# A hand-laid order for VectorE and ScalarE in the first two blocks of a retention-plus-MLP kernel

## The chip, the cores and the metric

The kernel runs on one core of a Trainium2 chip. The time of a kernel is the device time of one execution in microseconds (us); medians and ranges over several executions are given. A run counts as slow when it takes over 1.5% longer than the fastest of the same kernel; every timed run told here was in the other, fast state, except one single look whose state can't be known and from which no total time is compared. "The profile" is one recorded execution. Its engines are TensorE (PE, with its weight loads as PEld), VectorE (DVE), ScalarE (ACT), GpSimd (POOL) and SyncE (SP).

## The reference

```python
# attention: batch 4, 8 heads, 768 steps, head_dim 64
gamma = 1.0 - 2.0 ** (-5.0 - np.arange(H))
for t in range(S):
    state = gamma * state + einsum('bhd,bhe->bhde', k[:, :, t], v[:, :, t])
    y[:, :, t] = scale * einsum('bhd,bhde->bhe', q[:, :, t], state)
# bridge: x is (3072 tokens, 512);  w_in (512, 2048), w_out (2048, 512), both float64
h = x @ w_in
g = h * (1.0 / (1.0 + np.exp(-1.702 * h)))
out = g @ w_out
```

The kernel works on the recurrence in chunks of 64 steps of two batches at once, 128 rows. A chunk needs transposes of q and k ("turn"), masked scores, values, a carried state and a sum into X ("attend"). The weights come as float64 and are converted to float32 on the chip.

## The kernel before

Only the first 115 us of some 690 concern us. In them the kernel does eight chunks of attention, the 16 first-layer units of block one (`up0`), and the conversion of `w_in` (`narrow`), all interleaved. A unit is called (h, p): h is the half of block one's tokens, p the slice of the weights.

```python
def narrow():                                   # converts one slice of float64 weights
    ...
    tc.keep_in_program_order(act.activation(m, hi.bitcast(F32), AF.Abs, scale=2.0 ** 16))
    tc.keep_in_program_order(dve.tensor_scalar(m, m, ...))
    dve.tensor_scalar(mu, mu, 3, ...)
    dve.scalar_tensor_tensor(hi, hi, 0x80000000, mu, ...)
    dve.tensor_scalar(mu, hi, 0xFF800000, ...)
    dve.scalar_tensor_tensor(lo.bitcast(F32), lo, 2.0 ** -52, m, ...)
    dve.tensor_add(w, hi, lo)
    ...

def decay(j):                                   # k of a chunk, scaled for the state
    ...
    keep(pool.tensor_mul(KD[j], QKV.pop(("kn", j)), cold[:, H:2 * H, None].to_broadcast([P, H, D])))

def attend(j, f=None):
    ...                                         # matmuls into pa (scores, state) and py (values)
    dve.tensor_mul(AT[j], pa[:, :, 0], mask)
    ...
        dve.tensor_mul(tmp, py[:, :, 1]..., rowd...)     # row decay
        dve.tensor_add(x, y, tmp...)                     # the sum into X
    ...
        pool.tensor_mul(new, old, whole...)              # state decay
        dve.tensor_add(new, new, u)

def hidden(g, h):                               # frees the unit's PSUM tile
    act.activation(s, h, AF.Sigmoid, scale=1.702)
    ...
        dve.tensor_mul(g, h[:, i], s[:, i])

def up0(half, p, tag):
    h = ps.tile([P, 2, TH], F32, name="ph", tag=tag)
    ...                                         # the matmuls of one unit
    hidden(...)

# the schedule
for n, unit in enumerate([(1, p) for p in range(3)] + [(half, p) for p in range(3, NP) for half in range(2)]):
    up0(*unit, "xxyx"[n % 4])
    if n % 2 == 0:
        narrow()
    if n in (1, 4, 7, 10):
        between.pop(0)()
for f in range(NFF):
    up1(f)                                      # block two
```

Most instructions on DVE and ACT aren't kept in program order here: a scheduler lays them. After block two's units come the second layer and the remaining blocks, where PE is full.

Of the kernel before, what the change touches and what calls it, by code (L numbers as in the profile page):

```python
# [13 lines left out]
P = 128  # L14
# [14 lines left out]
def kernel(  # L29
# [66 lines left out]
    rowd = const.tile([P, HP, D], F32, name="rowd")  # L96
    cold = const.tile([P, 2 * H], F32, name="cold")
# [3 lines left out]
    state = [const.tile([P, 2, HP, D], F32, name=f"state{i}") for i in range(2)]  # L101

# [3 lines left out]
    def load(j, what="qkv"):  # L106



        b, c = j // NC * 2, j % NC  # L110
        rows = slice(c * D, (c + 1) * D)

        def plain(name, src, tag, bufs, engine=sp):
            t = two.tile([P, H, D], F32, name=name + "_in", tag=tag, bufs=bufs)
            QKV[name, j] = t
            for i in range(2):
                engine.dma_start(t[i * D:(i + 1) * D], src[b + i, :, rows, :].rearrange("h p d -> p h d"))

        if j < 2 * CB:
            if "q" in what:  # L120
                plain("q", q, "q_sq", 2)
                plain("kn", k, "k_sq", 2, sp if j else act)
        elif "q" in what:
            for name, src in (("q", q), ("k", k)):
                t = two.tile([P, HP, P // C4, C4], F32, name=name + "_sq")
                for r0 in range(0, P, C4):
                    d0, h0 = r0 % D, r0 // D * HP
                    for n in range(P // C4):
                        t0 = c * D + n * C4 % D
                        tc.keep_in_program_order(sp.dma_start(  # L130
                            t[r0:r0 + C4, :, n], src[b + n * C4 // D, h0:h0 + HP, t0:t0 + C4, d0:d0 + C4]
                            .rearrange("h p d -> p h d")))
                QKV[name, j] = t
        if "v" in what:
            if j >= 2 * CB and c < NC - 1:
                plain("kn", k, "kn", 1)
            plain("v", v, "v", 2)
# [15 lines left out]
    def fetch():  # L153
        i = fetched[0]
        if i < len(SRC):
            x = raw(i).rearrange("p (n two) -> p n two", two=2)
            sp.dma_start(x.rearrange("p (c f) two -> p c f two", c=2) if i < NFF else x, SRC[i])
            fetched[0] = i + 1

    narrowed = [0]  # L160

    def narrow():


        i = narrowed[0]
        if i == len(SRC):
            return
# [21 lines left out]
        dve.tensor_scalar(mu, mu, 3, None, op0=ALU.logical_shift_left)  # L189
        dve.scalar_tensor_tensor(hi, hi, 0x80000000, mu, op0=ALU.bitwise_and, op1=ALU.bitwise_or)  # L190
        dve.tensor_scalar(mu, hi, 0xFF800000, None, op0=ALU.bitwise_and)  # L191
        dve.scalar_tensor_tensor(lo.bitcast(F32), lo, 2.0 ** -52, m, op0=ALU.mult, op1=ALU.mult)  # L192
        lo, hi = lo.bitcast(F32), hi.bitcast(F32)
        if i < NFF:
            lo, hi = [t.rearrange("p (c ab f) -> p c ab f", ab=2, f=P) for t in (lo, hi)]
        dve.tensor_add(w, hi, lo)  # L196
        for _ in range(n):
            fetch()
# [17 lines left out]
    def turn(j):  # L216

        QT[j], KT[j] = home(j, "qT"), home(j, "kT")
        if j < 2 * CB:
            x = QKV.pop(("q", j)), QKV["kn", j]  # L220
            p = [ps.tile([P, 2, HP, D], F32, name="pt", tag="y") for i in range(2)]
            order = [(n, s, i, r) for n in range(2) for s in range(HP) for i, r in TWO]
            for n, s, i, r in sorted(order, key=lambda o: o[2]) if j == 0 else order:
                pe.matmul(p[i][HALF[r], n, s, :], x[n][HALF[i], HP * r + s, :], ident[HALF[i], HALF[i]],
                          start=True, stop=True)
            t = G[:, 0:2, j % 2 * 2:j % 2 * 2 + 2, :].rearrange("p n a t -> p n (a t)").rearrange(
                "p n (s t) -> p n s t", s=HP)
            for i in range(2):
                act.activation(t[:, :, :, HALF[i]], p[i], AF.Copy)
            decay(j)  # L230
        else:
            for t, name in ((QT[j], "q"), (KT[j], "k")):
                tc.keep_in_program_order(dve.transpose(
                    t.rearrange("p h t -> p (h t)"), QKV.pop((name, j)).rearrange("p h s d -> p (h s d)")))
        if j + 2 < NCH and (j + 2 < 2 * CB or j >= 2 * CB):
            load(j + 2, "qk")

    def decay(j):
# [4 lines left out]
        keep = tc.keep_in_program_order if j == 0 else lambda i: i  # L243
        keep(pool.tensor_mul(KD[j], QKV.pop(("kn", j)), cold[:, H:2 * H, None].to_broadcast([P, H, D])))  # L244

    def attend(j, f=None):
# [33 lines left out]
        if j is not None:  # L280
            AT[j] = home(j, "at")
            dve.tensor_mul(AT[j], pa[:, :, 0], mask)  # L282
            if j > 2 * CB:
                decay(j)
        if f is not None:
            half, t0 = f % CB // 2, f % 2 * D
            x = X1 if f // CB == 1 else X
            x = x[:, 2 * half:2 * half + 2].rearrange("p r s (i t) -> p (r s) i t", i=2)[:, :, :, t0:t0 + D]
            by = "p i r (s t) -> p (r s) i t"
            y = py[:, :, 0].rearrange(by, t=D)  # L290
            if c:
                tmp = two.tile([P, 2, 2, P], F32, name="tmp", bufs=1)
                dve.tensor_mul(tmp, py[:, :, 1].rearrange("p r i t -> p i r t"),
                               rowd.rearrange("p (r s) t -> p r (s t)", r=2)[:, None].to_broadcast([P, 2, 2, P]))
                dve.tensor_add(x, y, tmp.rearrange(by, t=D))
            else:
                act.activation(x, y, AF.Copy)
            u = pa[:, :, 1]
            if c == 0:
                dve.tensor_copy(new, u)  # L300
            elif c < NC - 1:
                pool.tensor_mul(new, old, whole[:, None, :, None].to_broadcast([P, 2, HP, D]))  # L302
                dve.tensor_add(new, new, u)  # L303
            if f + 2 < 2 * CB:
                load(f + 2, "v")
# [4 lines left out]
    def hidden(g, h):  # L310

        s = two.tile([P, 2, TH], F32, name="sg")
        act.activation(s, h, AF.Sigmoid, scale=1.702)  # L313
        for g, i in g if isinstance(g, list) else [(g, slice(0, 2))]:
            dve.tensor_mul(g, h[:, i], s[:, i])  # L315
# [12 lines left out]
    def up0(half, p, tag):  # L328

        h = ps.tile([P, 2, TH], F32, name="ph", tag=tag)  # L330
        for ab in range(2):
            for c in range(4):
                w = W1[:, p, 2 * ab + c // 2, c % 2, :]
                pe.matmul(h[:, ab], w, X[:, 2 * half + c // 2, c % 2, :], start=(ab == 0 and c == 0), stop=(c == 3),  # L334
                          skip_group_check=True)
        if half == 0:
            hidden(W1[:, p, 4:6].rearrange("p s c f -> p s (c f)"), h)
        else:
            hidden([(g1(0, p, 2 + i), i) for i in range(2)], h)
# [131 lines left out]
    load(0, "qk")  # L471
    make_identity(nc, ident)
    W = col_decay.shape[1]
    m3 = mask.rearrange("p r h t -> p (r h) t")
    for i in range(2):

        pool.dma_start(cold[HALF[i]].rearrange("p (n h) -> p n h", n=2),
                       bass.AP(tensor=col_decay.tensor, offset=col_decay.offset, ap=[[W, D], [D * W + H, 2], [1, H]]))
    pool.dma_start(m3, bass.AP(tensor=row_decay.tensor, offset=row_decay.offset, ap=[[0, P], [P, H], [1, D]]))
# [4 lines left out]
    fetch()  # L484
    load(0, "v")
    fetch()
    load(1)
    idle = ps.tile([P, HP, P], F32, name="idle", tag="x")

    def keep_warm(n):  # L490

        for _ in range(n):
            pe.transpose(idle[:, 0, :], ident, ident)


    for o in range(2):
        act.activation(rowd[HALF[o]], m3[HALF[o], o:H:2, :], AF.Copy)

    dve.tensor_mul(m3, m3, cold[:, 0:H, None].to_broadcast([P, H, D]))
    for i in range(2):  # L500
        pool.affine_select(out=m3[HALF[i]], in_=m3[HALF[i]], compare_op=ALU.is_ge, fill=0.0, base=0,
                           pattern=[[0, H], [1, D]], channel_multiplier=-1)
# [5 lines left out]

    keep_warm(7)
    narrow()  # L510
    turn(0)

# [4 lines left out]
    attend(0)  # L517
    narrow()
    for _ in range(2):
        fetch()  # L520
    turn(1)
    attend(1, 0)
    for _ in range(2):
        fetch()
    turn(2)
    for j in range(2, 5):
        attend(j, j - 1)
        turn(j + 1)
        narrow()
        up0(0, j - 2, "x")  # L530
    between = [lambda j=j: (attend(j, j - 1), turn(j + 1)) for j in (5, 6)] + [lambda: attend(7, 6), lambda: attend(None, 7)]
    for n, unit in enumerate([(1, p) for p in range(3)] + [(half, p) for p in range(3, NP) for half in range(2)]):
        up0(*unit, "xxyx"[n % 4])
        if n % 2 == 0:
            narrow()
        if n in (1, 4, 7, 10):
            between.pop(0)()
    for f in range(NFF):
# [3 lines left out]
        if f >= NFF - 4:  # L542
            sums_w2(2 * (f - NFF + 4))
        if f >= NFF - 2:
            load(2 * CB + f - NFF + 2, "qkv" if f == NFF - 2 else "qk")
    for m in range(NB):
# [12 lines left out]
        for n, unit in enumerate(down(m)):  # L559
            unit()  # L560
            if m == 0 and n < NP // 2:
                sums_w2_t3(2 * n)
# [52 lines left out]
```

## Time and profile before

| | kernel before |
|---|---|
| median (range) | 694.2 us (691.48 to 697.53, 4 runs) |
| profiled span | 692.5 us |
| PE busy, share of the span | 670.6 us, 97% |
| DVE, ACT, POOL busy | 53%, 18%, 21% |
| block two's units begin | 113.75 us |

The shares are averages over the whole span; what matters is the stage that has holes. Span less PE busy is 21.9 us, and 16.5 of that lie in the first 52.40 us, where PE was busy for 35.90.

### The profile page before, as it was taken

What the parts mean: (1) busy time and instruction counts of PE and PEld (TensorE: products, weight loads), DVE (VectorE), ACT (ScalarE), POOL (GpSimd) and SP (SyncE); (2) the same over time, 40 slices, a digit from 0 to 9 for tenths busy, and PEclk for the clock granted to TensorE, in tenths of its full rate; (3) what the DMA queues carried; (4) which work ended last, traced back from release to release, by engine and by line L of the source; (5) the groups of instructions that cost most, each with busy time, mean ns of one, the idle gap of its engine ahead of it and who ended that gap; (6) DMA issues with size and microseconds to landing.
All of it is one profiled execution on the core that took longest, in us unless ns stands there. A gap on an engine that the chain in (4) does not pass through costs nothing.

```text
span 692.5 us, 14320 instructions
## 1 busy us (share of the span) xinstructions
PE 670.6 (97%) x6087; PEld 562.0 (81%) x6087; DVE 368.7 (53%) x512; ACT 127.7 (18%) x201; POOL 145.2 (21%) x131
## 2 busy tenths in 40 slices
PE   5779999999999999999999999999999999999997
PEld 4668886445888888888888888888888888888886
DVE  3499999997341563344373445373345373344241
ACT  3232323331000000332000333000233000233000
POOL 4221200000168343100244100244200143000030
PEclk9999999999999999999999999999999999999999
DMA  8875544422212213310323320223320220000001
GB/s 199 220 194 169 160 147 137 168 50 32 41 20 57 66 29 76 74 36 4 68 36 87 74 43 2 58 48 88 74 42 1 45 50 31 17 0 1 16 0 46
DMA packets 140368, 46.85 MB, mean 68 GB/s; under 512 B 131792, under 2 KB 132816, under 8 KB 140304
## 3 DMA queue, kind: packets, MB, share of 16 engines
q1 hardware_dynamic: 136352, 39.10, 24.6%
q0 software_dynamic: 1808, 5.52, 2.2%
q10 hardware_dynamic: 2144, 1.31, 0.6%
q8 instruction: 48, 0.79, 0.5%
q14 instruction: 16, 0.13, 0.1%
HBM read 39.59 MB, written 6.29 MB: 66 GB/s over the span
## 4 chain that ended last, share of the span: by engine, by line
PE 84%; DVE 11%; DMA 3%; issue 1%; POOL 0%; ACT 0%; ACTq 0%; SPq 0%; POOLq 0%
PE pd L439 39%; PE px L386 16%; PE py L386 12%; PE ph L347 8%; PE ph L334 3%; DMA kn_in<-in_k_dram 3%; PE pa L252 2%; PE py L278 1%; PE py L272 1%; DVE W L196 1%; PE pa L263 1%; DMA whole<-in_col_decay_dram 1%; DVE W L189 1%; DVE W L192 1%; DVE W L191 1%
## 5 line engine op out<-in xcount | busy, mean ns | idle before, releaser
L439 PE MATMUL pd<-W,G 128*128 128x256 f32 x1120 | 247.4, 381 | 0.4 <-DVE G L377 0.3
L439 PEld LDWEIGHTS pd<-W,G 128*128 128x128 f32 x1120 | 211.3, 190 | 30.3 <-DVE G L377 1.2
L386 PE MATMUL px<-X,W 128*128 128x256 f32 x512 | 119.0, 379 | 0.0
L386 PEld LDWEIGHTS px<-X,W 128*128 128x128 f32 x512 | 97.3, 190 | 13.2
L386 PE MATMUL py<-X,W 128*128 128x256 f32 x384 | 90.7, 379 | 0.0
L386 PEld LDWEIGHTS py<-X,W 128*128 128x128 f32 x384 | 73.0, 190 | 9.9
L334 PE MATMUL ph<-X,W 128*128 128x256 f32 x256 | 59.8, 394 | 5.9 <-DVE W L196 5.3
L334 PEld LDWEIGHTS ph<-X,W 128*128 128x128 f32 x256 | 50.0, 198 | 13.7 <-DVE W L196 5.5
L244 POOL TENSOR_TENSOR kd<-kn_in,cold 128x512 f32<-128x512 f32 x14 | 17.2, 1225 | 188.1 <-PE pa L263 161.3
L347 PE MATMUL ph<-W,W 128*128 128x512 f32 x128 | 55.2, 593 | 0.3 <-DVE W L315 0.3
L347 PEld LDWEIGHTS ph<-W,W 128*128 128x128 f32 x128 | 24.2, 190 | 30.8 <-issue 29.7
L378 POOL TENSOR_TENSOR G<-G 128x512 f32<-128x512 f32 x20 | 29.5, 1482 | 91.9 <-DVE G L377 90.4
L282 DVE TENSOR_TENSOR at<-pa,mask 128x512 f32<-128x512 f32 x16 | 11.0, 686 | 62.1 <-PE pa L263 53.6
L315 DVE TENSOR_TENSOR G<-G,sg 128x512 f32<-128x512 f32 x48 | 33.0, 688 | 14.0 <-ACT sg L313 14.0
L431 POOL DMA_DIRECT2D out_dram<-o x20 | 14.9, 746 | 121.2 <-DVE o L430 121.2
L313 ACT ACTIVATE sg<-G 128x512 f32<-128x512 f32 x48 | 30.2, 630 | 51.3 <-DVE G L396 30.7
L439 PE MATMUL pd<-W,W 128*128 128x256 f32 x160 | 35.8, 381 | 0.4 <-DVE W L377 0.3
L302 POOL TENSOR_TENSOR state<-state,whole 128x512 f32<-128x512 f32 x20 | 22.0, 1098 | 66.0 <-DVE state L303 60.5
L313 ACT ACTIVATE sg<-ph 128x512 f32<-128x512 f32 x32 | 19.1, 598 | 88.4 <-PE ph L334 40.8
L439 PEld LDWEIGHTS pd<-W,W 128*128 128x128 f32 x160 | 30.2, 190 | 5.6 <-DVE W L377 1.2
L396 DVE TENSOR_TENSOR G<-py,p 128x512 f32<-128x512 f32 x16 | 11.1, 692 | 37.8 <-PE py L386 37.8
L426 ACT ACTIVATE u<-pd 128x512 f32<-128x512 f32 x6 | 3.6, 597 | 135.6 <-PE pd L439 135.6
(105 smaller groups left out, 659.0 us busy)
## 6 DMA issues: line engine op xcount, KB each, us to landing
W<-in_moe_w_in_dram SPq DMA_DIRECT2D x12, 512.0 KB, 5.6
v_in<-in_v_dram SPq DMA_DIRECT2D x48, 128.0 KB, 3.3
kn_in<-in_k_dram SPq DMA_DIRECT2D x42, 128.0 KB, 3.2
W<-in_moe_w_out_dram SPq DMA_DIRECT2D x10, 512.0 KB, 4.1
out_dram<-o POOLq DMA_DIRECT2D x20, 256.0 KB, 2.7
q_sq<-in_q_dram SPq DMA_DIRECT2D x256, 16.0 KB, 1.9
k_sq<-in_k_dram SPq DMA_DIRECT2D x256, 16.0 KB, 1.8
G<-in_moe_w_out_dram SPq DMA_DIRECT2D x6, 512.0 KB, 5.1
```

The source lines that it names most:

```text
L244: keep(pool.tensor_mul(KD[j], QKV.pop(("kn", j)), cold[:, H:2 * H, None].to_broadcast([P, H, D])))
L252: pe.matmul(pa[HALF[i], r, 0, s, :], KT[j][HALF[r], s, HALF[i]], QT[j][HALF[r], s, HALF[i]], start=True, stop=True)
L302: pool.tensor_mul(new, old, whole[:, None, :, None].to_broadcast([P, 2, HP, D]))
L313: act.activation(s, h, AF.Sigmoid, scale=1.702)
L315: dve.tensor_mul(g, h[:, i], s[:, i])
L334: pe.matmul(h[:, ab], w, X[:, 2 * half + c // 2, c % 2, :], start=(ab == 0 and c == 0), stop=(c == 3), skip_group_check=True)
L347: pe.matmul(h, w, X1[:, c // 2:4:2, c % 2, :], start=(c == 0), stop=(c == 3))
L378: pool.tensor_sub(a[1], a[1], a[0])
L386: pe.matmul(acc[:, u, :], W1[:, 2 * d + u, sa, c, :], X[:, sb, c, :], start=(start and u == 0 and c == 0), stop=(stop and c == 1), skip_gr ...
L396: dve.tensor_add(a[0], y, p1)
L431: (pool if m < NB - 1 else act).dma_start(rows[th, e], o)
L439: pe.matmul(p0[:, n, :], g1(m, p, sa)[:, n * P:(n + 1) * P], W2[:, sb, p, :], start=(new and p == 0 and n == 0), stop=(last and p == NP - ...
```

## The change

Its intent: fill PE's early holes. The instructions of DVE and ACT in the first two blocks get a fixed order (`pin`). Conversions are split into halves that can be placed between other work. The row decay is multiplied into q during its transposes, through a diagonal matrix in place of the identity. Both decays move from GpSimd to eight and four small ScalarE activations. Loads come earlier, some warming matmuls are counted anew, and W2's sums move behind block two. The core of the diff:

```diff
+    ordered = [True]
+    def pin(i):
+        return tc.keep_in_program_order(i) if ordered[0] else i
...
+    def half():
+        if second: second.pop()()
+        else: first_half()
...
-                pe.matmul(p[i][HALF[r], n, s, :], x[n][...], ident[HALF[i], HALF[i]],
+                pe.matmul(p[i][HALF[r], n, s, :], x[n][...],
+                          ident[HALF[i], HALF[i]] if n or j == 0 else diag[HALF[i], HP * r + s, :],
...
-        keep(pool.tensor_mul(KD[j], QKV.pop(("kn", j)), cold[:, H:2 * H, None].to_broadcast([P, H, D])))
+            for h in range(H):
+                tc.keep_in_program_order(act.activation(KD[j][:, h], x[:, h], AF.Copy, scale=d[:, h]))
...
+                    for s in range(HP):
+                        pin(act.activation(new[:, :, s], old[:, :, s], AF.Copy, scale=whole[:, s:s + 1]))
...
-        hidden(W1[:, p, 4:6]..., h)                 # inside up0: at once
+        return lambda: hidden(W1[:, p, 4:6]..., h)  # when the schedule calls it
...
+    u = up0(0, 2, "x")
+    half()
+    u()
+    attend(None, 3)
...
-        up0(*unit, "xxyx"[n % 4])
-        if n % 2 == 0:
-            narrow()
-        if n in (1, 4, 7, 10):
+        half()
+        done, u = u, up0(*unit, "xxyx"[n % 4])
+        done()
+        if n in (0, 1, 3, 5, 7, 9):
             between.pop(0)()
...
+        if f == 1:
+            dve.tensor_mul(m3, m3, rows("x"))
```

`done` is the hidden product of the unit issued one step earlier.

## The prediction

> **What bounds the kernel now.** I read the page's busy slices first, then a table of stretches, then the timeline and the chain of waits. The slices show which stage can still give time:
>
> ```profile
> PE   5779999999999999999999999999999999999997
> PEld 4668886445888888888888888888888888888886
> DVE  3499999997341563344373445373345373344241
> ACT  3232323331000000332000333000233000233000
> ```
>
> A slice is 17.3 us. TensorE (PE) has gaps only in the first four slices and is at 9 afterwards. VectorE (DVE) is at 9 through slices 3 to 9, ScalarE (ACT) never above 3. The change edits the stage up to about slice 7 (blocks one and two: eight chunks of attention, 16 up-projection units of 512 columns, conversion of w_in). The stretches, columns being length, then busy time with instruction count of PE, weight load, DVE, ACT and GpSimd (POOL), then granted clock, DMA share and GB/s:
>
> ```profile
> 0.00:52.40 52.40, 35.90 (x936) 31.47 (x936) 30.93 (x41) 15.06 (x24) 16.35 (x22) 0.96 0.81 203
> 52.40:113.75 61.35, 60.41 (x832) 52.40 (x832) 58.42 (x80) 16.50 (x24) 8.95 (x7) 0.98 0.52 156
> 113.75:168.95 55.20, 55.20 (x129) 24.58 (x130) 52.38 (x69) 15.71 (x22) 0.00 (x0) 1.00 0.35 95
> ```
>
> Before 52.4 us PE has holes and DMA is the busiest (0.81); from 52.4 to 113.75 PE and DVE are both full. The chain of waits (start, length, work) has these pieces:
>
> ```profile
> 24.66 6.64 DMA kn_in<-in_k_dram
> 31.34 1.06 PE pt L224 x28
> 32.40 4.90 PE ph L334 x16
> ...
> 52.37 12.07 PE ph L334 x48
> ...
> 113.75 55.20 PE ph L347 x128
> ```
>
> So the first unit starts at 32.40, behind the transposes of chunk 3, whose k landed late; only two of 16 units are done by 52.37, and block two's own units (L347) start at 113.75. From there to the end, 579 us, PE is full and its work hardly changes. The prediction is therefore one number: when does L347 start in the changed kernel?
>
> Costs, from the timeline: one unit of 16 matmul records is a third of 10.36 us, 3.45 (48 records of equal width in the chain take 10.36); a group of 32 small matmuls advances PE by 0.47, so a chunk is 0.94 of transposes (turn), 0.47 of scores and 1.41 of values. That makes 16 x 3.45 + 8 x 2.82 = 78 us, so 26 of the first 104 us after start-up are holes. A conversion pair on DVE:
>
> ```profile
> 73.56 0.69 DVE L187 TENSOR_SCALAR W<-W 128x1024 f32<-128x1024 f32 x1 [0.28 <-ACT W L186]
> 74.29 0.69 DVE L189 TENSOR_SCALAR W<-W 128x1024 uint32<-128x1024 uint32 x1
> 75.02 1.23 DVE L190 SCALAR_TENSOR_TENSOR G<-G,W 128x1024 uint32<-128x1024 uint32 x1
> ```
>
> Start to start these give 0.73 + 0.73 + 1.16 = 2.62 for the first half, and the three that follow (0.71, 1.26, 1.14) 3.11 for the second.
>
> **What the Trainium skill says.** (1) "SBUF — State Buffer", Who interferes with whom: DVE and GpSimd arbitrate for one port pair, as an exclusive lock. The trace agrees:
>
> ```profile
> 44.57 1.49 POOL L244 TENSOR_TENSOR G<-kn_in,cold 128x512 f32<-128x512 f32 x1
> 45.20 1.42 DVE L189 TENSOR_SCALAR W<-W 128x1024 uint32<-128x1024 uint32 x1
> ```
>
> beside each other both are slow (1.04 and 0.69 alone). (2) "ScalarE: Activation LUTs", What ACT_TABLE_LOAD costs: an ACTIVATE takes 186 ns + 0.833 ns per element, 93 more for each per-partition pointer, and neighbours overlap by 93. The trace agrees on the pointer-free form (0.60 for 512 out of PSUM); none with a pointer is in it. Estimate from that page: eight of 64 elements 8 x 0.24 + 0.09 = 2.0 us; four of 128 elements 1.25 us. (3) "TensorE: Matmul & The Clock Gate", Part 1: about 3.4 us of idling halves the array clock. Agrees: after 3.39 us of waiting, 48 records at 52.37 took 12.07 instead of 10.36.
>
> **The change, part by part.**
> Removed from DVE: the row-decay product in seven of eight chunks (7 x 0.60 start to start = 4.2 us; chunk 0 gains one). Its factor goes into q's transposes as a diagonal, free on PE, and the plain copy moves to ACT, 0.5 each. Removed from POOL: eight products of 1.04 to 1.53 and seven state products of 1.04, about 16 us off the critical path, but they slowed DVE perhaps 3 to 4 us in all. Added on ACT per chunk: 2.0 + 1.25 + 0.5 = 3.75 us, 28 us over the stage; with 1.0 of transposed copies, 1.13 of conversion input and two sigmoids of 0.5 ACT has about 7.4 us per chunk. Removed from the start: the broadcast load of the row decay (256 KB). Moved: loads of chunks 2 and 3 earlier, the units ahead of the later chunks, W2's sums behind L347. Added in L347: one 512-wide matmul and a 0.6 us product, some 0.4 to 0.9 us on full PE. Everything on DVE and ACT is now in fixed order.
>
> The early part, walked by hand on the printed order of instructions. k of chunk 0 lands at about 8 (8.67 now, with less beside it); scores and both first conversions keep DVE busy; the value sum of chunk 0 reaches X at 19.6, chunk 1 at 22.2. First unit 22.2 against 32.4: ten us ahead. Then DVE leads: second conversion pair ends 29.5, unit two runs 29.5 to 33.0; chunk 3's q and k have 7.1 MB ahead of and in them, at some 205 GB/s they land near 35.5; chunk 2's values, the fixed order of conversion four (5.7), a hidden product and chunk 3's addition put X complete at 49.7. PE idles 44.5 to 49.7. Then three units of the second half and one more end at 66.8, with seven units done (the old kernel has five at 68.1 but two more groups of attention).
>
> The later part, where I expect the lead to go. A unit's PSUM tile is one of two in its tag, and is free only after its hidden product on DVE. The new order puts that product behind: values on PE 1.88 + 0.27, tmp on ACT 0.5, state scaling 1.25, transposed copies 1.0, decay 2.0, conversion input 1.1, first half conversion 2.62, product 0.65: 11.3 us after the unit's end. PE's own work in that time is 1.88 + 0.94 + 3.45 = 6.3. So PE should idle 5 us after unit (1,3), 1.6 us before unit (1,4), 3 us before unit (0,6). From 49.75: 13 units 44.9, attention 11.3, waits 5 + 1.6 + 3 + 0.9 = 10.5; L347 starts at about 116.4, not 113.75. That is +2.6, with +0.6 for the rows matmul, and up to 1.7 of slow clock after each of two long waits. Against this I hold 3 us: the order and its counted warming matmuls look tuned on a chip, so some of my waits are probably too long. Sum: 694.4 + 2.6 + 0.6 + 1.5 - 3, rounded to 695.5.
>
> **The rivals.**
> One: the ten us lead survives. If the ACT decays overlap better, or sums leave their tiles sooner, only the 5 us before X is complete remain: 49.7 + 44.9 + 11.3 = 106, minus 2 if chunk 3 lands sooner. L347 at 104 to 106, time 684 to 687. For it: ACT was at 3 tenths, DVE gets rid of 4 us plus the port conflicts. Against: the product order above is fixed, no scheduler may mend it.
> Two: ACT becomes the bound. If the small activations do not overlap, eight cost 2.6 and four 1.55, +0.9 per chunk on a chain that is crossed about six times, and PE falls cold in each hole: L347 at 122 to 126, time 703 to 707. For it: two row-decay copies of 256 elements took 0.84 together, no overlap seen.
> Three: DMA hides it. The loads share 203 GB/s before 52.4; if chunk 3 or the third conversion pair lands later than 35.5, the first units' lead of ten us shrinks to 5, and L347 moves by what X's completion moves, 2 to 3 us: 697 to 699.
>
> **Range and chances.** Walked centre 116.4 with 4 us on either side from the early chain, 4 from ACT's unmeasured small operations, and rival one as a tail below: 684 to 704, eight in ten. Faster by 2% needs 680.5, L347 at 99.9, which is 6 us less than PE's work without a single wait after my 49.7: one in ten, as my 49.7 may be late. Slower by 2% needs 708.3, L347 at 127.6: one in twenty.
>
> **What would show it.** Right: the first unit near 22, X complete (first unit of the second half) near 50, PE waits of 3 to 5 us before units (0,4) and (0,6) released by the hidden product on DVE, DVE waits on the conversion input of ACT (four or so, 2 to 4 us each), the eight decay activations about 2 us together, DVE's fixed-scalar steps at 0.69 throughout, L347 at 112 to 120, and the rest 579 us long. Wrong: L347 below 106 or above 124; no PE wait on the hidden product; a later stage (W2's sums now behind L347) that no longer runs PE full.

## The result, and the profile after

The changed kernel took 714.68 us (median; 713.28 to 716.7, 4 runs) against 694.2 us. The ratio is 1.0295, with a 95% interval from 1.0243 to 1.0347. Ratios in this document are the mean time of one kernel's fast runs over that of the other's of the same rounds, so not quite the ratio of the medians. The change made the kernel slower by 3%, and 714.68 lies outside the predicted range of 684 to 704.

The profiled span is 713.7 us, 21.2 more than before. PE is busy for 679.7 us, 9.1 more, and idle for 34.0, 12.1 more. The busy slices of the page, after (a digit is a tenth of a slice of 17.8 us):

```profile
PE   7678798899999999999999999999999999999997
PEld 6567677444688888888888888888888888888886
DVE  3765758899652175244373344383344383344241
ACT  4554444132100000133100143100133100233000
```

PE's first slice is fuller than before (7, was 5), but slices 2, 4, 5, 7 and 8 are emptier, down to 7 and 8 where there was 9. ACT rose from 2 or 3 to 4 or 5, so it is half idle. DVE fell in slices 3 to 8 from 9 to between 5 and 8: it is no longer full, yet PE isn't full either. When no engine is full, each is waiting for another in turn. The stretches, with the columns of the prediction's table:

```profile
0.00:52.40 52.40, 39.16 (x846) 33.07 (x846) 30.62 (x44) 26.33 (x69) 6.31 (x15) 0.90 0.74 204
52.40:113.75 61.35, 48.61 (x821) 41.05 (x822) 41.29 (x57) 26.72 (x69) 0.00 (x0) 0.92 0.45 129
113.75:168.95 55.20, 52.01 (x238) 28.52 (x238) 48.24 (x60) 16.76 (x25) 1.04 (x1) 0.97 0.35 109
```

The second stretch carries the loss. PE was busy there for 60.41 us, now 48.61, and DVE fell from 58.42 to 41.29. The granted clock fell as well, from 0.98 to 0.92. The early rise of PE's busy time, from 35.90 to 39.16, is partly the same work done more slowly (the granted clock fell from 0.96 to 0.90) and not more work. Next, the units that waited, from the timeline of PE after (start, length, line, operation, records, and in brackets the idle time before and what released it):

```profile
25.79 3.72 PE L376 MATMUL ph<-X,W 128*128 128x256 f32 x16 [0.16 <-DVE X L340]
33.33 6.67 PE L376 MATMUL ph<-X,W 128*128 128x256 f32 x16 [2.73 <-DVE W L222]
...
55.20 6.00 PE L376 MATMUL ph<-X,W 128*128 128x256 f32 x16 [4.76 <-DVE X L340]
...
87.38 5.27 PE L376 MATMUL ph<-X,W 128*128 128x256 f32 x16 [3.77 <-DVE W L357]
...
112.63 3.69 PE L376 MATMUL ph<-X,W 128*128 128x256 f32 x16 [2.75 <-DVE W L357]
...
131.87 8.65 PE L388 MATMUL ph<-W,W 128*128 128x512 f32 x16 [3.19 <-DVE W L357]
```

In order these are units (0,0), (0,1), (1,0), (0,4) and (0,6), and the first group of block two (L388). A unit that isn't slowed takes 3.69 to 3.72 us here. In the first 3.3 us of (0,1) the granted clock was 0.50, so "slow" below means a slow clock. L222 is the end of a conversion, L340 the sum into X, and L357 the hidden product that frees a PSUM tile. The first unit is 6.6 us earlier than before; block two is 18.1 us later (131.87 against 113.75). The rest, from there to the end, is 581.8 us against 578.75.

One piece of the chain that ended last, after (start, length, work), shows what (0,4) waited for:

```profile
81.23 1.66 ACT G L276 x7
82.89 1.03 ACT W L210
83.95 0.70 DVE W L211
84.68 0.70 DVE W L213
85.41 1.23 DVE W L214
87.38 5.27 PE ph L376 x16
```

The key decay on ACT (L276) stands ahead of the conversion input (L210), that ahead of DVE's half conversion (L211 to L214), and that ahead of PE's unit. The timeline after has what goes before and between:

```profile
77.45 0.60 ACT L337 ACTIVATE tmp<-py 128x512 f32<-128x512 f32 x1 [4.86 <-PE py L312]
77.95 1.26 ACT L344 ACTIVATE state<-state,whole 128x128 f32<-128x128 f32 x4
...
80.89 2.01 ACT L276 ACTIVATE G<-kn_in,cold 128x64 f32<-128x64 f32 x8
...
86.55 0.68 DVE L357 TENSOR_TENSOR W<-ph,sg 128x512 f32<-128x512 f32 x1
```

The product at 86.55 is that of unit (0,3), whose matmuls ended at 75.36 (68.19 plus 7.17 for two units in one group). It ends at 87.23, and PE goes on at 87.38. So a finished tile stayed occupied for 11.9 us, while work that has nothing to do with it was done on ACT and DVE.

### The profile page after: what moved, and what is told of

Its sections match the earlier page's. It is cut to its first block, busy times and chain, and to the rows that moved or that the text cites. A ratio compares the mean times of both kernels' runs of the same rounds, so it can differ in the third digit from the quotient of the medians.

```text
span 713.7 us, 14499 instructions
## 1 busy us (share of the span) xinstructions
PE 679.7 (95%) x6144; PEld 565.4 (79%) x6144; DVE 364.2 (51%) x508; ACT 153.8 (22%) x300; POOL 126.4 (18%) x118
## 4 chain that ended last, share of the span: by engine, by line
PE 87%; DVE 9%; ACT 2%; issue 1%; DMA 1%; SPq 0%; POOL 0%; ACTq 0%; POOLq 0%
PE pd L480 38%; PE px L427 15%; PE py L427 12%; PE ph L388 8%; PE ph L376 5%; PE pa L286 2%; PE py L312 1%; PE pt L253 1%; PE pa L297 1%; PE py L306 1%; DVE W L214 1%; DVE W L211 1%; ACT W L210 1%; DVE W L218 1%; ACT state L344 1%; DVE W L213 1%
## 5 line engine op out<-in xcount | busy, mean ns | idle before, releaser
L427 PEld LDWEIGHTS px<-X,W 128*128 128x128 f32 x512 | 97.3, 190 | 13.2
L376 PE MATMUL ph<-X,W 128*128 128x256 f32 x256 | 65.4, 416 | 16.3 <-DVE W L357 6.5
L376 PEld LDWEIGHTS ph<-X,W 128*128 128x128 f32 x256 | 52.4, 209 | 26.7 <-issue 10.5
L388 PE MATMUL ph<-W,W 128*128 128x512 f32 x128 | 57.0, 607 | 3.2 <-DVE W L357 3.2
L388 PEld LDWEIGHTS ph<-W,W 128*128 128x128 f32 x128 | 24.8, 195 | 34.9 <-issue 30.0
L419 POOL TENSOR_TENSOR G<-G 128x512 f32<-128x512 f32 x20 | 29.5, 1482 | 91.8 <-DVE G L418 91.8
L357 DVE TENSOR_TENSOR G<-G,sg 128x512 f32<-128x512 f32 x48 | 33.0, 688 | 13.7 <-ACT sg L355 13.7
L346 POOL TENSOR_TENSOR state<-state,whole 128x512 f32<-128x512 f32 x13 | 13.5, 1040 | 119.9 <-DVE state L347 119.6
```

The costliest lines, as they stand in the source:

```text
L346: pool.tensor_mul(new, old, whole[:, None, :, None].to_broadcast([P, 2, HP, D]))
L357: pin(dve.tensor_mul(g, h[:, i], s[:, i]))
L376: pe.matmul(h[:, ab], w, X[:, 2 * th + c // 2, c % 2, :], start=(ab == 0 and c == 0), stop=(c == 3), skip_group_check=True)
L388: pe.matmul(h, w, X1[:, c // 2:4:2, c % 2, :], start=(c == 0), stop=(c == 3))
L419: pool.tensor_sub(a[1], a[1], a[0])
L427: pe.matmul(acc[:, u, :], W1[:, 2 * d + u, sa, c, :], X[:, sb, c, :], start=(start and u == 0 and c == 0), stop=(stop and c == 1), skip_gr ...
```

## The experiments

Each run is told with its edit against the changed kernel unless another is named. Medians of the kernel before in the same rounds were between 693.27 and 693.82 us.

### e1_warm: keep the clock up in four waits

Four units ran slowly right after a wait. If their slow clock is the cause, harmless matmuls in those waits should give the time back.

```diff
+        if n: spin(h.rearrange("p a t -> p (a t)"), n)      # up0, before the unit's own matmuls
-    u = up0(0, 1, "x")
+    u = up0(0, 1, "x", 11)                                  # pairs of dummy matmuls
+        if n == 5: spin_pa(14)                              # before (0,4)
-        done, u = u, up0(*unit, "xxyx"[n % 4])
+        done, u = u, up0(*unit, "xxyx"[n % 4], 19 if n == 0 else 0)
+    spin_pa(12)                                             # before block two
```

> The changed kernel with 11 to 19 pairs of dummy matmuls put into four waits of TensorE (before units (0,1), (1,0), (0,4) and the first unit of block two). Nothing waits less, only the array stays busy. Theory A (the waits cost twice, because the units behind them run at half clock): those four units go from 6.67, 6.00, 5.27 and 8.65 (two units) back to 3.5, 3.5, 3.5 and 6.9, so about 9 us are saved: 704 to 707. Rival C (the waits alone are the loss, the slow units lie beside other waiting): 712 to 715. If the dummies overrun their holes: above 715.

Measured: 712.76 us (709.96 to 713.87, 4 runs), ratio 1.0264. The four groups did run at full speed: (0,1), (1,0) and (0,4) took 3.72, and block two's first 7.13 instead of 8.65. That is 2.95 + 2.28 + 1.55 + 1.52 = 8.3 us less. But block two began no earlier. From the timeline of PE in this run:

```profile
93.70 8.86 PE L378 MATMUL ph<-X,W 128*128 128x256 f32 x32 [0.68 <-ACT G L259]
...
110.91 5.38 PE L378 MATMUL ph<-X,W 128*128 128x256 f32 x16 [2.68 <-DVE W L357]
...
131.84 7.13 PE L390 MATMUL ph<-W,W 128*128 128x512 f32 x16 [0.42 <-DVE W L357]
```

Two later groups became slow in their place (8.86 was 7.17 and 5.38 was 3.69, 3.4 us together), and a new wait of 2.3 us, for which the profile names no releaser, appeared among the matmuls of a turn. Up to (0,4) this run was ahead, 83.78 against 87.38 us, although its first unit had begun 0.6 us later (26.40 against 25.79). The new slow groups and the new wait then took the lead away, so that block two began within 0.03 us of the changed kernel's is a coincidence. The run thus moved slow work more than it removed it, and it doesn't show what a full clock would be worth. It shows that filling these four waits is no remedy. Its time fits rival C (712 to 715) without proving it. Against the kernel before of its own rounds the gain is 1.1 us (19.4 in place of 20.5), within the scatter of the runs.

### e2_product_first: the hidden product ahead of the half conversion

One line of the loop moves. Nothing else changes, neither the number of tiles nor the work.

```diff
-        half()
         done, u = u, up0(*unit, "xxyx"[n % 4])
         done()
+        half()
```

> The changed kernel with one line moved: in the loop of 13 units the hidden product of the last unit comes before the next half conversion, not after it. Theory A (a PSUM tile is held until the product behind conversion input and half conversion): the waits before unit (0,4) and before block two shrink by 3.7 and 3.2 us, the one before (0,6) goes, and the slow clock after two of them: 701 to 706. Rival B (the decays on ScalarE are the loss): 711 to 715. Rival D (fixing the order at all is the loss): 711 to 715.

Measured: 700.62 us (699.78 to 701.53, 4 runs), ratio 1.0096. That is 14.1 us less than the changed kernel (13.2 if each is taken against the kernel before of its own rounds), and just below the 701 to 706 expected. Its timeline of PE:

```profile
33.34 3.69 PE L376 MATMUL ph<-X,W 128*128 128x256 f32 x16 [2.72 <-DVE W L222]
...
52.60 5.41 PE L376 MATMUL ph<-X,W 128*128 128x256 f32 x16 [4.86 <-DVE X L340]
...
80.94 3.69 PE L376 MATMUL ph<-X,W 128*128 128x256 f32 x16 [0.71 <-DVE W L357]
...
117.97 7.13 PE L388 MATMUL ph<-W,W 128*128 128x512 f32 x16 [0.24 <-DVE W L357]
```

The wait before (0,4) fell from 3.77 to 0.71 us and that before block two from 3.19 to 0.24, so block two came 13.9 us earlier. Of the slow groups only (1,0), at 5.41, is left.

Not all of this is the edit's. Up to unit (1,0) the two programs issue the same instructions in the same order. Yet (0,1) took 6.67 us in the changed kernel and 3.69 here after the same wait, and (1,0) began at 52.60 instead of 55.20. These 2.6 us of the 13.9 come from the clock in one profile. From (1,0) to block two the changed kernel took 76.67 us, and 78.88 in a second profile (e12, 53.99 to 132.87); e2 took 65.37. Taking off what slow groups took too long in that stretch (3.8, 6.1 and 1.7 us) leaves, as an estimate, 72.8, 72.8 and 63.7: the moved line is worth some 9 us of waits, and the rest of the gain is slow work that wasn't there. By the medians this one line is about two thirds of the loss against the kernel before (20.5 us). It isn't the whole loss.

### e3_decays_pool: decays back on GpSimd

```diff
-            for h in range(H):
-                tc.keep_in_program_order(act.activation(KD[j][:, h], x[:, h], AF.Copy, scale=d[:, h]))
+            tc.keep_in_program_order(pool.tensor_mul(KD[j], x, d.to_broadcast([P, H, D])))
-                    for s in range(HP):
-                        pin(act.activation(new[:, :, s], old[:, :, s], AF.Copy, scale=whole[:, s:s + 1]))
+                    pin(pool.tensor_mul(new, old, whole[:, None, :, None].to_broadcast([P, 2, HP, D])))
```

> The changed kernel with both decays (keys and state) back on GpSimd as in the kernel before, all else kept. Rival B (decays on ScalarE are the loss): back to 694 to 699. Theory A: the chain to the PSUM tile loses 2.0 to 3.3 us per crossing, and VectorE's steps beside GpSimd get longer again: 705 to 711.

Measured: 711.91 us (711.18 to 712.62, 4 runs), ratio 1.0262, 2.8 us less than the changed kernel. The wait before (0,4) fell from 3.77 to 1.95 us and that before block two from 3.19 to 2.37, but the first unit began at 28.30 instead of 25.79. The decays make the bad chain longer; they aren't why it is there.

### e4_unpinned: the scheduler's order

```diff
-    ordered = [True]
+    ordered = [False]
```

> The changed kernel with the order of VectorE and ScalarE left to the scheduler again (only what was fixed before is fixed). Rival D (the fixed order is the loss): 694 to 700. Theory A: the scheduler has the same order of issue to choose from, with decays and conversion input still in a row on ScalarE; it only lifts single products: 706 to 715.

Measured: 706.98 us (706.42 to 708.01, 4 runs), ratio 1.0189. The scheduler's order of the same instructions beats the hand-laid one by 7.7 us, and is 6.4 us worse than the hand-laid one with one line moved. Its own flaw, from the timeline of PE:

```profile
93.33 9.59 PE L376 MATMUL ph<-X,W 128*128 128x256 f32 x32 [6.36 <-ACT G L259]
```

It put transposed copies (L259) late on ACT, and PE waited 6.36 us at one place. So fixing the order isn't wrong in itself.

### e5_x_early: e2, with chunk 3's values ahead of the second half of conversion four

The longest wait left in e2 is that of unit (1,0), 4.86 us for X (L340).

```diff
     half()
     u = up0(0, 2, "x")
-    half()
-    u()
     attend(None, 3)
     load(5, "v")
+    half()
+    u()
```

> Product first (as in e2) and, one step earlier, chunk 3's values are summed before the second half of conversion four and the hidden product of unit (0,2), not after them. Theory A (what is left of the loss after e2 is again something TensorE waits for, standing behind conversions in the fixed order): the wait before unit (1,0), 4.86 us in e2, shrinks by 3.1 + 0.6 us, and block two starts 3 to 6 us sooner than e2's 117.97: 694 to 698. If the chunk were late for another reason (loads): 699 to 702.

Measured: 695.04 us (694.43 to 695.75, 4 runs), ratio 1.0024 (0.9999 to 1.0048), 5.6 us less than e2. Its unit (1,0), from the timeline of PE:

```profile
49.06 3.72 PE L376 MATMUL ph<-X,W 128*128 128x256 f32 x16 [1.44 <-DVE X L340]
```

It starts 3.5 us earlier than in e2, and isn't slow any more. Block two begins at 112.81, 5.2 us earlier. The late X had nothing to do with data that came late: DVE did a conversion first.

### e6_reordered: e5, with two further moves at the start

```diff
-    turn(0)
     rd = rows("x")
+    turn(0)
...
-    attend(None, 1)
-    half()
+    attend(None, 1, half)
```

> e5 and two more moves: the first half of conversion three goes where VectorE waits for chunk 1's values (2.7 us in e2), and the row decay's matmul goes ahead of the first transposes instead of behind them. Theory A: unit (0,1) can start 3 us sooner, the scores of chunk 0 about 1 us sooner; together with e5 block two starts at 108 to 113 (kernel before 113.75): 687 to 693, a little faster than the kernel before. If TensorE's own clock or the loads hold the start: 694 to 698.

Measured: 698.32 us (696.37 to 699.2, 6 runs), ratio 1.0062: a miss, 3.3 us worse than e5. The rows matmul now stood ahead of the first transposes and waited 2.73 us for the load of the row decay; the first unit began at 29.09 instead of 25.48. Two edits in one run can't say which of them did it. e10 and e15 separate one of the two.

### e7_row_decay_undone: e2, with the row decay out of q's turn

```diff
-                          ident[HALF[i], HALF[i]] if n or j == 0 else diag[HALF[i], HP * r + s, :],
+                          ident[HALF[i], HALF[i]],
...
-                if f < 2 * CB:
-                    pin(act.activation(tmp, z, AF.Copy))
-                else:
-                    dve.tensor_mul(tmp, z, scale)
+                pin(dve.tensor_mul(tmp, z, scale))
...
     rd = rows("x")
+    pin(dve.tensor_mul(m3, m3, rd))
...
-        if f == 1:
-            dve.tensor_mul(m3, m3, rows("x"))
```

> e2 with the row decay taken out of q's turn again: the mask holds it from the start, VectorE multiplies the old-state part by it in each chunk (7 products of 0.60 more, one less), no diagonal, no matmul of rows in block two. If the row decay's move pays as intended: VectorE has 3.6 us more and the start loses nothing, 702 to 705. If the rows matmul (1.1 us in block two, about 2 us at the start) eats the gain: 697 to 701.

Measured: 697.35 us (697.11 to 698.28, 4 runs), ratio 1.0059, 3.3 us less than e2. From its timeline of PE:

```profile
22.61 3.72 PE L371 MATMUL ph<-X,W 128*128 128x256 f32 x16 [0.81 <-DVE X L335]
```

The first unit begins 3.2 us earlier than in e2 (25.80), although DVE now does the row product again. Part of that is a faster clock at the start of this profile: chunk 0's scores began at 9.54 here and at 11.27 in e2. In e15, which starts like e2 (11.26), the first unit begins at 23.39, 2.4 us earlier. Block two begins at 116.21, 1.8 us earlier, and the rest lasts 578.8 us instead of 580.3, since the rows matmul and its product no longer stand in block two (1.8 + 1.5 = 3.3). So putting the row decay into q's turn was a loss, in part by way of the work ahead of the first unit.

### e8_before_decays_act: the kernel before, with both decays on ScalarE

```diff
# against the kernel before; no pin, no other change
-        keep(pool.tensor_mul(KD[j], QKV.pop(("kn", j)), cold[...]...))
+            for h in range(H):
+                keep(act.activation(KD[j][:, h], x[:, h], AF.Copy, scale=d[:, h]))
...
-                pool.tensor_mul(new, old, whole...)
+                    for s in range(HP):
+                        act.activation(new[:, :, s], old[:, :, s], AF.Copy, scale=whole[:, s:s + 1])
```

> The kernel before with one part of the change alone: both decays on ScalarE in the first two blocks, in the scheduler's order. Rival B (the decays on ScalarE are the loss): above 703. Theory A: they do little by themselves, ScalarE has room and VectorE loses the port conflicts: 690 to 698.

Measured: 706.7 us (705.88 to 711.23, 4 runs), ratio 1.0205. In the scheduler's order the move alone costs 13 us. One place where it shows, from this run's timeline:

```profile
75.37 0.40 ACT L309 ACTIVATE state<-state,whole 128x128 f32<-128x128 f32 x1 [3.60 <-DVE state L312]
75.68 1.06 ACT L229 ACTIVATE G<-pt 128x512 f32<-128x512 f32 x2
76.31 13.26 PE L343 MATMUL ph<-X,W 128*128 128x256 f32 x48 [4.42 <-ACT G L229]
```

ACT stood idle for 3.60 us because its next instruction, a state scaling, waited for DVE's state. The transposed copies behind it (L229) were held up with it, and PE waited 4.42 us for those. In the kernel before the same wait stands on GpSimd, and not ahead of the copies.

### e9_product_first_pool: e2 and e3 together

The edit is the sum of those of e2 and e3.

> Both undone: product first (e2) and both decays back on GpSimd (e3). Fourth corner of the square of changed kernel 714.7, e2 700.6, e3 711.9. If the two losses add up: 697 to 699. If the decays only cost through the chain that the late product made (so nothing is left of them once it is early): 700 to 702. If the decays on ScalarE are worth what they cost in the kernel before (13 us in e8): 686 to 690.

Measured: 700.56 us (696.62 to 701.41, 4 runs), ratio 1.0076. Against e2's 700.62 the runs show no difference between the two places of the decays, once the product is where it should be.

### e10_all_moves and e11_all_moves_pool: the moves together

e10 is e7 with e5's move and with the half conversion moved into chunk 1's values, as in e6. e11 is the same with the decays on GpSimd.

```diff
# against e7
-    attend(None, 1)
-    half()
+    attend(None, 1, half)
...
     u = up0(0, 2, "x")
-    half()
-    u()
     attend(None, 3)
     load(5, "v")
+    half()
+    u()
```

> Product first, chunk 3's values early (e5), row decay undone (e7), and the first half of conversion three in VectorE's wait for chunk 1's values (that part of e6 without the early rows matmul, which in e6 waited 2.7 us for its load). Decays stay on ScalarE, the order stays fixed. If e5's and e7's gains add (695.0 less 3.3) and the moved half saves 1 to 3 us: 688 to 692, faster than the kernel before by up to 0.8%. If the middle stretch is bound by something else: 693 to 696.

> e10 with both decays on GpSimd: what is then left of the change is the fixed order with halves, and the order of loads. If the decays on ScalarE still cost: 2 to 5 us below e10. If GpSimd's port conflicts with VectorE cost more: 1 to 4 us above e10.

Measured: e10 694.71 us (692.15 to 696.32, 6 runs), ratio 1.0009 (0.9976 to 1.0042); e11 695.64 us (692.13 to 696.89, 6 runs), ratio 1.0019. Neither can be told from the kernel before, so the 688 to 692 hoped for were missed. The start of e10, from the timeline of PE:

```profile
26.75 5.37 PE L371 MATMUL ph<-X,W 128*128 128x256 f32 x16 [3.66 <-DVE X L335]
```

The half conversion within chunk 1's values delayed the sum that the first unit waits for: 26.75, where e7 had 22.61 (with its faster start) and e15, the same program without the moved half, has 23.39.

### e12_changed_again: the changed kernel once more

The edit is a comment line. The question was whether the slow units are always the same ones.

> The changed kernel once more, one profile. In its first profile unit (0,1) ran at half clock (6.67 us) and in e2, with the same work in the 26 us before it and the same 2.7 us wait, at full clock (3.69). If the clock there is chance: near 3.7 here or between, with block two starting up to 3 us sooner, and the whole at 711 to 716. If it is fixed by the schedule: 6.6 to 6.7 again.

Measured: 716.3 us, one profile, state unknown. Three of its units, from the timeline of PE (line numbers are one higher by the comment):

```profile
32.74 5.38 PE L377 MATMUL ph<-X,W 128*128 128x256 f32 x16 [2.08 <-DVE W L223]
...
53.99 5.31 PE L377 MATMUL ph<-X,W 128*128 128x256 f32 x16 [4.86 <-DVE X L341]
...
112.06 5.27 PE L377 MATMUL ph<-X,W 128*128 128x256 f32 x16 [2.76 <-DVE W L358]
```

In the first profile these three took 6.67, 6.00 and 3.69 us. The later waits stayed what they were (2.75 and 2.76 before (0,6)), while the slow groups differ from one run to the next.

### e13_before_key_decay_act and e14_before_state_decay_act: which decay costs e8 its 13 us

Each is one half of e8's edit to the kernel before: the key decay alone, and the state decay alone.

> The kernel before with the key decay alone on ScalarE, eight activations, in the scheduler's order. Theory (the state scaling is what costs, because it waits for VectorE's state ahead of the transposed copies): the key decay waits only for its own inputs, so 692 to 698 us. Rival (ScalarE's load as such costs, and the key decay is the longer of the two, 2.0 against 1.26 us): 699 to 704 us.

> The kernel before with the state scaling alone on ScalarE. Theory: most of the 13 us of both decays comes back with this one, 700 to 706 us, and the trace shows PE waiting for the transposed copies (G) behind a state scaling that waits for VectorE's state. Rival (load as such): under 699 us, less than the key decay costs.

Measured: e13 697.85 us (695.46 to 699.53, 4 runs), ratio 1.0047; e14 698.78 us (698.07 to 700.09, 4 runs), ratio 1.0059. Each costs 4 to 5 us against 693.82. The theory that the state scaling carries most of it has fallen: 698.78 is below the 700 to 706 it asked for, and the two are nearly equal. The rival, load as such with the key decay the costlier, doesn't fit either, as e13 stayed below its 699. Together the two cost 13 us and singly 4 and 5, so some 4 us come only from both being there. In e8 the place shown above has a state scaling waiting right after a key decay of 2.03 us in ACT's order; in e14 the longest such wait of a unit on the copies is 0.76 us. The step that the theory names does occur in e14, but early and without lasting effect: PE's scores at 25.03 us waited 2.39 us for copies behind a state scaling (0.58 in the kernel before), and the first unit still began at 31.45, no later than before (32.33). That the two make each other worse is measured; by which step they do is not settled.

### e15_three_undone and e16_three_undone_pool: three parts undone

e15 is e10 without the moved half conversion: the product first (e2), chunk 3's values first (e5), and the row decay out of q's turn (e7). e16 has the decays on GpSimd besides.

```diff
# e15 against e10
-    attend(None, 1, half)
+    attend(None, 1)
+    half()
```

> The changed kernel with the product before the half conversion, chunk 3's values before the second half of conversion four, and the row decay out of q's turn; decays stay on ScalarE. If the three parts add: 700.6 less 5.6 (values early) less 3.3 (row decay) is 691.7, so 690 to 694 us, first unit at 22.6, block two at 109 to 112 us. If they overlap, since either lets the same units start earlier: 694 to 696 us.

> As e15, with both decays on GpSimd. Hand-laid order alone then remains of the change. If ScalarE is the better place for the decays: 1 to 3 us slower than e15. If the place is worth nothing once the order is right: within 1 us of e15.

Measured: e15 692.39 us (690.32 to 693.08, 6 runs), ratio 0.9968 (0.9943 to 0.9993); e16 692.34 us (691.21 to 693.53, 6 runs), ratio 0.997 (0.9945 to 0.9995). From e15's timeline of PE:

```profile
23.39 3.72 PE L371 MATMUL ph<-X,W 128*128 128x256 f32 x16 [0.94 <-DVE X L335]
...
47.44 3.72 PE L371 MATMUL ph<-X,W 128*128 128x256 f32 x16 [1.54 <-DVE X L335]
...
111.21 39.32 PE L383 MATMUL ph<-W,W 128*128 128x512 f32 x91 [0.59 <-DVE W L352]
```

The parts add, as far as runs can be compared: e5's 5.6 and e7's 3.3 taken from e2's 700.62 give 691.7, and 692.39 was measured. Every unit of block one took its full-speed 3.7 us in that profile, and the granted clock of the run was 1.000. Again no difference between the two places of the decays can be seen. In e16's profile two units were slow (4.22 and 5.41 us), and its time is the same. Both kernels beat the kernel before and the changed one; against the kernel before it is by 0.3%, below what counts as faster here (2%), but the intervals leave 1 out. The gain over e10, 2.3 us, is measured on two chips, so only its sign and the earlier first unit (23.39 against 26.75) are relied on.

## Why the prediction was wrong

**What held.** The structure and the mechanism were right. A single number decides, the start of block two; the rest of the kernel is nearly the same length (581.8 against 578.75 us). The decisive chain was named and its size was right: 11.3 us from a unit's end to the release of its tile were predicted, 11.9 were measured. So were the waits it makes. Predicted 5 us before (0,4), measured 3.77; predicted 3 before (0,6), measured 2.75. The 1.6 predicted before (1,4) met a wait of 1.41 by luck: it was released by the transposed copies, and it is still 1.41 in e2, where the product comes early. From the Trainium skill ("ScalarE: Activation LUTs", What ACT_TABLE_LOAD costs) the prediction estimated 2.0 us for eight small activations with a per-partition pointer and 1.25 for four; 2.01 and 1.26 were measured. PE idled 4.76 us ahead of X, with 5.2 predicted. Rival one, a lead that survives, was rightly held unlikely for the order as written. Rival two's premise, 2.6 and 1.55 us for those activations, failed by the same measurement. ACT does hold up others by its decays, but in the scheduler's order (e8), not mainly in the hand-laid one (e3). Rival three, the loads, found no support: the waits that decide are all released by DVE or ACT.

**Where the 15.5 us are.** The walk put block two at 116.4; it began at 131.87. By the walk's own steps:

- The early part. The first unit was to start at 22.2 and started at 25.79; unit (0,1) was to start at 29.5 and started at 33.33. That is 3.8 us. The walk has no matmul for the rows at the start (its 0.4 to 0.9 us are those of the one in block two); this one took 2.07 us ahead of chunk 0's scores, as the timeline after shows:

```profile
9.27 2.07 PE L550 MATMUL rows<-G 1*128 1x512 f32 x2
```

  Chunk 0's sum, foreseen in X at 19.6, was there at 22.31: DVE did it behind a half conversion, and PE waited 1.49 us for it. The next group of 32 small matmuls then took 0.90 us to advance in place of 0.47, with the granted clock at 0.50; in e12 it took 0.52. Without the row decay in q's turn, but with that rows matmul, the first unit started at 23.39 (e15).
- From there to (1,0). That unit was to start at 49.7 and started at 55.20, 5.5 us late. Of these 3.8 are from before, and 1.7 are new: (0,1) took 2.95 us more than a full-speed unit, so the rest of this stretch was a little shorter than walked.
- From (1,0) to the end of (0,3): 17.1 us by the walk, 20.2 measured. Of the 3.1 us more, 2.28 are the slow (1,0).
- From there to block two: 49.6 us by the walk, 56.5 measured. Of the 6.9 us more, 3.19 are a wait that the walk left out: block two's first group needs a tile whose product stands behind a half conversion, exactly as in the units before. Another 1.55 are the slow (0,4). In the other 2.2 us, a wait of 1.32 within a turn (at 78.81; the profile puts it down to the state scaling on ACT) is outweighed by the three predicted waits, together 1.7 us shorter than predicted; some 2.5 us are spread over units and chunks that each took a little longer than the walk's 3.45 and 2.82.

The sum is 3.8 + 1.7 + 3.1 + 6.9 = 15.5 us. On top of this, the 3 us that the prediction took off because the order "looks tuned on a chip" were not there. The rest of the kernel grew by 3.1 us where the prediction allowed 0.6 (its 1.5 for the slow clock belonged to waits before block two); 1.5 of it are the rows matmul and its product by e7, and 1.5 the slow first group of block two.

**The step that failed** is thus not the mechanism but three terms of the sum: the early chain (3.8 us too little), the slow clock after waits (1.5 allowed; 8.3 counted in four groups), and the omitted wait for block two (3.19), with a credit of 3 us for which the profile had no line. All of them erred to the same side. How large the clock term is in one profile is partly chance (e12).

The working also has slips that don't decide the result. Its sum as written gives 696.1, not 695.5. PE is below 9 in three of the early slices (5, 7, 7), not in four. And its 26 us of holes mix holes with slow work and dummy matmuls: by its own table PE was idle for 17.4 us before block two (16.5 + 0.9).

**What the cause is.** The kernel is slower because DVE and ACT have a fixed order in which an instruction that frees a PSUM tile stands behind a half conversion that doesn't need to be first. This is shown by e2: one line moved, 14.1 us back, the wait before (0,6) gone and that before (0,4) down to 0.71. By the estimate from the profiles some 9 us of it are waits; the rest is slow work, of which 2.6 us lie before the moved line can act. A further 5.6 us are the sum into X standing behind the other half conversion (e5), and 3.3 the row decay's way through q's turn (e7). They leave 692.39 when all are undone (e15), 22.3 us less than the changed kernel and 1.4 less by the medians than the kernel before. How far the slow clock follows from the waits is not shown: with four waits filled, other groups were slow (e1); e15, with short waits, had no slow unit, but e16, with waits as short, had two.

**What stays open.** The earlier loads, the new count of warming matmuls and the move of W2's sums were never undone by themselves; e15 and e16 keep them. Why a unit is slow after one wait and not after another of the same length: (0,1) took 6.67 us after 2.73 in the changed kernel and 3.69 after 2.72 in e2. Why the two decays on ScalarE cost more together than singly in the kernel before. And which of e6's two moves did how much of its harm.

## What to carry to other kernels

When the order of an engine is fixed by hand, put the instruction that frees a tile of a scarce pool, or completes the input of the busiest engine, ahead of long work that nobody waits for yet; walk each tile from its last write to its release, and don't forget the first tile of the stage that follows. Moving work to an idle engine isn't free: in e8 an instruction that waited 3.60 us on ACT stood ahead of copies for which PE then waited 4.42. Leave room in the sum for slow work after waits (8.3 us in one profile here), and take no credit for tuning that no line of the profile shows. And before a difference between two profiles is put down to an edit, look whether it begins where the edit can act: 2.6 us of e2's didn't.

## What the Trainium skill lacked or had wrong

- "TensorE: Matmul & The Clock Gate", Part 1: it ties the slow clock to about 3.4 us of idling, and says of a kernel's start that the window is free-running and the number of slow matmuls varies by run; it also tells of a kernel slowed by frequent short idles, without their length. Here, in the middle of a kernel, units were slow after less than 3.4 us: 6.67 us after a wait of 2.73, and 5.38 after 2.08, where a full-speed unit takes 3.7. The prediction's own chain has one, 4.90 us at 32.40, with a wait of 2.26 before the transposes ahead of it. The same wait gave a full-speed unit in e2 (3.69 after 2.72), so the length of the wait alone doesn't predict it in this kernel. The page lacks a warning that filling waits can move slow work elsewhere: four groups lost 8.3 us of it, two others gained 3.4 (e1).
- "Perfetto Trace Analysis", Optimization Strategy: it says that consistent bubbles can mean that there isn't enough SBUF or PSUM for the next tile, and names the count and size of buffers. It doesn't name the order of the instruction that frees a tile. Moving it by one line took 3.77 us of waiting down to 0.71 with no tile added (e2). Whether a further tile would have done the same was not tried.
- No page says when GpSimd is as good a place for the decays as ScalarE: with the order right, 692.34 us (GpSimd) against 692.39 us (ScalarE), in e16 and e15.
